# Eight tiles with packed weights for the upper half of K, the lower half by natural weights that on-chip copies between partitions bring

## The chip, the cores and the metric

The kernel runs on one core of one Trainium2 chip. The metric is the device time of one execution in microseconds (us). "Before" took 235.51 us in three runs (235.48 to 235.56). A core has TensorE (called PE in the profile; PEld is its weight loading), VectorE (DVE), ScalarE (ACT), GpSimd (POOL) and SyncE (SP), and 16 DMA engines that move data. SPq and ACTq in the profile are the DMA queues that SyncE and ScalarE issue into.

Kernels are compared only within the same rounds. A ratio is the mean time of one kernel's fast runs over that of the other's of the same rounds, so it is not quite the ratio of the medians that are quoted.

## The reference

```python
# x (16, 512, 1024), w (1024, 1024), b (1024), all bf16
def reference(x, w, b):
    wg = w.reshape(256, 4, 1024)               # groups of 4 neighbours along K
    mag = abs(wg)
    thr = second_largest(mag, axis=1)          # (by argsort in the original)
    wp = (wg * (mag >= thr)).reshape(1024, 1024)   # 2 of 4 kept
    return einsum("bsd,df->bsf", x, wp) + b
```

So it is a matrix product of 8192 tokens with K = 1024 and 1024 output columns, with weights that are pruned two out of four first. The tokens make 64 tiles of 128.

## The kernel before

Pruning compares four neighbours along K. This kernel does it by elementwise operations with those four on the same partition (on VectorE from 3.8 to 26.0 us). For that the weights are loaded "packed": partition q of half g holds rows g*512 + 4q + m for m = 0..3. The other order is "natural": partition p of k-tile kt holds row kt*128 + p. Both orders give a right product, if x is arranged to match.

- *Packed tiles.* The first seven token tiles are multiplied with the packed weights as soon as a piece is pruned. Their x is transposed on TensorE by an identity matrix, in the packed order.
- *Natural tiles.* The other 57 tiles use natural weights; their x comes by transposing DMA loads, so TensorE only multiplies.
- *From packed to natural.* The pruned weights are saved to DRAM in the packed order and read back in the natural one.

```python
pieces = [(0, 0, 256), (0, 256, 512), (1, 0, 256), (1, 256, 512), (0, 512, 1024), (1, 512, 1024)]
...
def save(g, c0, c1, eng="sp"):                     # packed, to DRAM
    issue(eng, scr_pk[:, g, :, c0:c1], wp[:, g, :, c0:c1])
def reload(h):                                     # natural, from DRAM
    fs = slice(h * FH, (h + 1) * FH)
    sp(nc.sync.dma_start(wp_nat[:, :, fs], scr_nat[:, :, fs]))
def transpose(t, g):                               # x of a packed tile, on TensorE
    xg = x_sb[(t, g)].rearrange("p (q m) -> p m q", m=4)
    tp = psum_t.tile([P, 4, P], bf16, name="tp")
    for m in range(4):
        pe(nc.tensor.transpose(tp[:, m, :], xg[:, m, :], ident[:]))
...
def finish(t):                                     # VectorE adds the bias, twice for a packed tile
    o = outp.tile([P, Dout], bf16, name="o")
    dve(nc.vector.tensor_tensor(o[:, FH:], ps_open.pop((t, 1))[:], bias_sb[:, FH:], op=Alu.add))
    dve(nc.vector.tensor_tensor(o[:, :FH], staged.pop(t)[:], bias_sb[:, :FH], op=Alu.add))
    issue("act", of[t * P:(t + 1) * P, :], o[:])
...
run({eng: order[eng].split() for eng in order})    # written orders of pruning and packed tiles
save(0, 0, 256); save(0, 256, 512); save(1, 0, 256); save(1, 256, 512)
load_batch(0)                                      # transposing load of natural tiles
reload(0)
reload(1)
load_batch(1)
load_batch(2)
for t in (2, 0, 3, 1, 6, 5, 4):
    finish(t)
# ... then 57 tiles of 16 matmuls of 512 columns each (8 k-tiles, 2 column halves)
```

The helper `seq` ties the calls on one engine into the order of its instructions. An issue that takes long holds back those behind it in its queue.

## Time and profile before

| what | value | where it is read |
|---|---|---|
| time | 235.51 us (235.48 to 235.56, 3 runs) | times |
| span of the profiled run | 233.2 us | page |
| TensorE busy | 98% | page |
| a 512-column matmul | 176.12 us / 816 = 0.216 us | chain of waits |
| first packed matmul | 7.01 us | timeline |
| first natural matmul | 33.46 us | timeline |

The profile page of before. The first line is busy time, share of the span and count of each engine. The next four are groups of instructions: source line, engine, operation, output<-input, shapes, count, then busy us, mean ns of one, and the idle time of TensorE just before them. The last two are the shares of the chain of work that ended last.

```profile
PE 229.5 (98%) x1184; PEld 112.8 (48%) x1184; DVE 104.2 (45%) x177; ACT 15.2 (7%) x27; POOL 0.7 (0%) x6
...
PE 98%; DVE 0%; issue 0%
PE ps L394 76%; PE ps L219 10%; PE ps L359 9%; PE ps L131 2%; PE tp L194 2%; DVE o L363 0%; DVE zeros L80 0%
...
L394 PE MATMUL ps<-wp_nat,xb 128*128 128x512 bf16 x816 | 176.3, 379 | 0.0
...
L219 PE MATMUL ps<-wp,xt 128*128 128x256 bf16 (+1 forms) x168 | 25.5, 308 | 0.0
L359 PE MATMUL ps<-wp_nat,xb 128*128 128x512 bf16 (+2 forms) x112 | 21.1, 349 | 0.0
...
L194 PE MATMUL tp<-ident,x 128*128 128x128 bf16 x56 | 5.0, 227 | 0.0
```

Every group of matmuls has 0.0 us of idle time before it, and the chain is TensorE from end to end. (A single 512-column matmul is shown as 379 ns long, but they overlap: the pace is 216 ns.) L219 are the packed matmuls, L359 and L394 the natural ones, L194 the transposes, L131 fillers that multiply zeros before any weights are there.

The timeline of TensorE before: start us, length us, what ran. Rows between those shown are further transposes and packed matmuls.

```profile
7.01 1.47 PE L219 MATMUL ps<-wp,xt 128*128 128x256 bf16 x12
...
18.31 15.31 PE L219 MATMUL ps<-wp,xt 128*128 128x256 bf16 x84
33.46 17.43 PE L359 MATMUL ps<-wp_nat,xb 128*128 128x512 bf16 x80
```

The packed tiles last until 33.46 us. The timeline of SyncE's queue shows the conversion of the weights in the meantime; the length here is how long the issue keeps the queue.

```profile
10.55 6.84 SPq L92 DMA_DIRECT2D wp_scratch<-wp  x4
17.45 5.87 SPq L244 DMA_TRANSPOSE xb<-in_x_dram  x1
23.50 9.10 SPq L184 DMA_DIRECT2D wp_nat<-wp_scratch  x2
```

Saves, one transposing load, reloads: the left half of the natural weights landed at 29.5 us, behind 26 us of packed work, and the right half at 39.0 us, behind natural work. TensorE never waits for it: its idle time before L359 and L394 is 0.0 us.

### The profile page before, as it was taken

How to read it: one execution, taken by the hardware profiler on the slowest of the kernel's cores; microseconds unless marked ns; L12 is line 12 of the kernel's file. 1: busy time of each engine (PE TensorE's matmuls, PEld its weight loads, DVE VectorE, ACT ScalarE, POOL GpSimd, SP SyncE). 2: the span in 40 equal slices, each digit the busy share in tenths (PEclk: the TensorE clock that was granted, in tenths of full speed). 3: DMA queues.
4: the chain of work that ended last, by engine and by line, in shares of the span. 5: the costliest groups of instructions: out<-in, count | busy, mean ns of one | idle time of the engine just before them, and what ended most of it. 6: DMA issues, size and time to landing. Idle time of an engine off the chain costs nothing.

```text
span 233.2 us, 2871 instructions
## 1 busy us (share of the span) xinstructions
PE 229.5 (98%) x1184; PEld 112.8 (48%) x1184; DVE 104.2 (45%) x177; ACT 15.2 (7%) x27; POOL 0.7 (0%) x6
## 2 busy tenths in 40 slices
PE   8999999999999999999999999999999999999995
PEld 5987444444444444444444444444444444444443
DVE  3999559533343244244234334334324424423434
ACT  3679000000000000000000000000000000000000
POOL 1000000000000000000000000000000000000000
PEclk9999999999999999999999999999999999999999
DMA  6999969999999952992239921697221221122122
GB/s 189 297 327 248 322 214 224 282 257 247 241 340 258 273 166 88 209 285 94 90 74 253 257 91 46 146 239 202 90 90 49 88 93 63 72 90 91 47 89 90
DMA packets 79500, 40.29 MB, mean 173 GB/s; under 512 B 60416, under 2 KB 71936, under 8 KB 79488
## 3 DMA queue, kind: packets, MB, share of 16 engines
q1 hardware_dynamic: 68208, 22.32, 43.9%
q10 hardware_dynamic: 11280, 17.80, 22.9%
q8 instruction: 9, 0.15, 0.3%
q14 instruction: 3, 0.02, 0.0%
HBM read 6.29 MB, written 18.87 MB: 108 GB/s over the span
## 4 chain that ended last, share of the span: by engine, by line
PE 98%; DVE 0%; issue 0%
PE ps L394 76%; PE ps L219 10%; PE ps L359 9%; PE ps L131 2%; PE tp L194 2%; DVE o L363 0%; DVE zeros L80 0%
## 5 line engine op out<-in xcount | busy, mean ns | idle before, releaser
L394 PE MATMUL ps<-wp_nat,xb 128*128 128x512 bf16 x816 | 176.3, 379 | 0.0
L394 PEld LDWEIGHTS <-xb 128*128 128x128 bf16 x816 | 79.8, 98 | 96.3
L363 DVE TENSOR_TENSOR o<-ps,bias_sb 128x512 bf16<-128x512 f32 (+1 forms) x116 | 74.0, 677 | 117.2 <-PE ps L394 110.8
L219 PE MATMUL ps<-wp,xt 128*128 128x256 bf16 (+1 forms) x168 | 25.5, 308 | 0.0
L359 PE MATMUL ps<-wp_nat,xb 128*128 128x512 bf16 (+2 forms) x112 | 21.1, 349 | 0.0
L219 PEld LDWEIGHTS <-xt 128*128 128x128 bf16 x168 | 16.2, 98 | 7.5
L359 PEld LDWEIGHTS <-xb 128*128 128x128 bf16 x112 | 10.4, 98 | 10.7
L233 DVE TENSOR_TENSOR o<-ps,bias_sb 128x512 bf16<-128x512 f32 x7 | 4.8, 685 | 5.1 <-PE ps L219 5.1
L131 PE MATMUL ps<-zeros 128*128 128x128 bf16 (+1 forms) x32 | 5.3, 328 | 1.0 <-DVE zeros L80 1.0
L154 ACT ACTIVATE mag<-w_sb 128x1024 bf16<-128x1024 bf16 (+1 forms) x4 | 6.0, 1488 | 1.0 <-DMA w_sb<-in_w_dram 1.0
L151 DVE TENSOR_TENSOR wp<-w_sb,mag 128x1024 bf16<-128x1024 bf16 (+2 forms) x7 | 5.4, 766 | 0.2
L151 DVE TENSOR_TENSOR mag<-mag,hi 128x1024 bf16<-128x1024 bf16 (+2 forms) x7 | 5.3, 767 | 0.2
L199 ACT COPY xt<-tp 128x256 f32<-128x256 f32 x14 | 4.9, 372 | 5.3 <-PE tp L194 5.3
L194 PE MATMUL tp<-ident,x 128*128 128x128 bf16 x56 | 5.0, 227 | 0.0
L234 DVE TENSOR_TENSOR o<-st,bias_sb 128x512 bf16<-128x512 f32 x7 | 4.8, 679 | 0.0
L131 PEld LDWEIGHTS <-zeros 128*128 128x128 bf16 x32 | 3.0, 125 | 2.6 <-issue 1.7
L194 PEld LDWEIGHTS <-x 128*128 128x128 bf16 x56 | 4.0, 117 | 0.4 <-DMA x<-in_x_dram 0.2
L228 ACT COPY st<-ps 128x512 f32<-128x512 f32 x7 | 3.6, 609 | 0.1
L151 DVE TENSOR_TENSOR hi<-mag 128x512 bf16<-128x512 bf16 (+1 forms) x6 | 3.0, 507 | 0.0
L151 DVE TENSOR_TENSOR lo<-mag 128x512 bf16<-128x512 bf16 (+1 forms) x6 | 3.0, 508 | 0.0
L161 DVE TENSOR_SCALAR mag<-w_sb 128x1024 uint16<-128x1024 uint16 x2 | 0.9, 427 | 2.9 <-DMA w_sb<-in_w_dram 2.9
L151 DVE TENSOR_TENSOR hi<-hi,lo 128x256 bf16<-128x256 bf16 (+1 forms) x6 | 2.0, 336 | 0.2
(11 smaller groups left out, 6.4 us busy)
## 6 DMA issues: line engine op xcount, KB each, us to landing
out_dram<-o ACTq DMA_DIRECT2D x58, 256.0 KB, 3.9
wp_nat<-wp_scratch SPq DMA_DIRECT2D x2, 1024.0 KB, 6.4
x<-in_x_dram SPq DMA_DIRECT2D x5, 256.0 KB, 5.0
out_dram<-o ACTq DMA_DIRECT2D x10, 128.0 KB, 1.7
w_sb<-in_w_dram SPq DMA_DIRECT2D x4, 256.0 KB, 4.3
w_sb<-in_w_dram SPq DMA_DIRECT2D x2, 512.0 KB, 7.1
wp_scratch<-wp SPq DMA_DIRECT2D x4, 256.0 KB, 5.6
wp_scratch<-wp ACTq DMA_DIRECT2D x2, 512.0 KB, 5.2
```

Of the source, the lines that this page charges most:

```text
L131: pe(nc.tensor.matmul(warm_ps[:, :rep * P], lhsT=zeros[:], rhs=zeros[:, None, :].to_broadcast([P, rep, P]), start=True, stop=True))
L151: dve(nc.vector.tensor_tensor(out, a, b_, op=op))
L154: act(nc.scalar.activation(self.mag[:], self.w, Act.Abs))
L194: pe(nc.tensor.transpose(tp[:, m, :], xg[:, m, :], ident[:]))
L199: act(nc.scalar.copy(xt[:].bitcast(fp32), xpk[(t, g)][:].bitcast(fp32)))
L219: pe(nc.tensor.matmul(ps[:, c0 - h * FH:c1 - h * FH], lhsT=xpk[(t, g)][m], rhs=wp[:, g, m, c0:c1], start=(new and m == ms.start), stop=(le ...
L228: act(nc.scalar.copy(st[:], ps_open.pop((t, 0))[:]))
L233: dve(nc.vector.tensor_tensor(o[:, FH:], ps_open.pop((t, 1))[:], bias_sb[:, FH:], op=Alu.add))
L234: dve(nc.vector.tensor_tensor(o[:, :FH], staged.pop(t)[:], bias_sb[:, :FH], op=Alu.add))
L359: pe(nc.tensor.matmul(ps, lhsT=xt[:, kt, :], rhs=wp_nat[:, kt, c0:c1], start=(kt == 0), stop=(kt == KT - 1)))
L363: dve(nc.vector.tensor_tensor(o[:, c0:c1], ps, bias_sb[:, c0:c1], op=Alu.add))
L394: pe(nc.tensor.matmul(pss[h][:], lhsT=xt[:, kt, :], rhs=wp_nat[:, kt, h * FH:(h + 1) * FH], start=(kt == 0), stop=(kt == KT - 1)))
```

## The change

The intent is to take work from TensorE, which has none to spare. A packed tile costs transposes that a natural tile doesn't (56 for the seven tiles of before, 5.0 us of busy time). If the packed tiles use packed weights for the upper half of K only (g = 0) and natural weights for the lower half, then half of their transposes go. To keep TensorE busy while the rest of the weights are pruned and converted, there are eight such tiles instead of seven, and three natural tiles ("lead" tiles) begin with their upper half. The detour through DRAM was judged too slow for that (my estimate), so natural weights are copied from partition to partition on the chip. The upper-half sums are staged out of PSUM, in which the kernel has six buffers for sums: ScalarE copies 16 halves, GpSimd adds the bias to them, and VectorE later adds the staged half to the lower-half product.

The diff, cut to its core (cuts are marked `...`; the written orders of instructions and the loops over the natural tiles are left out):

```diff
-    NPK = 7
+    NPK = 8
+    LEAD = 3
...
-    def save(g, c0, c1, eng="sp"):
-        issue(eng, scr_pk[:, g, :, c0:c1], wp[:, g, :, c0:c1])
-    def reload(h):
-        fs = slice(h * FH, (h + 1) * FH)
-        sp(nc.sync.dma_start(wp_nat[:, :, fs], scr_nat[:, :, fs]))
+    def spread(g, c0, c1, eng="sp"):
+        for k in range(4):
+            issue(eng, wp_nat[:, 4 * g + k, c0:c1], wp[32 * k:32 * k + 32, g, :, c0:c1])
...
-    pieces = [(0, 0, 256), (0, 256, 512), (1, 0, 256), (1, 256, 512), (0, 512, 1024), (1, 512, 1024)]
+    pieces = [(0, 0, 256), (0, 256, 512), (0, 512, 768), (0, 768, 1024), (1, 0, 512), (1, 512, 1024)]
...
-    save(0, 0, 256)
-    ...
-    load_batch(0)
-    reload(0)
-    reload(1)
+    xnat = load_nat(NPK, NPK + LEAD, 0)        # transposing load, lead tiles, all of K
+    spread(0, 0, Dout)                         # upper half of K, natural
+    xnat.update(load_nat(0, NPK, 1))           # transposing load, packed tiles, lower half of K
+    spread(1, 0, FH)                           # lower half, left columns
+    spread(1, FH, Dout)                        # lower half, right columns
+    load_batch(0)
+    pruned = const.tile([P, 1], bf16)
+    pool(nc.gpsimd.tensor_copy(out=pruned[:], in_=wp[:, 1, 3, Dout - 1:]))   # after the last pruned piece
+    for tok in order["act"].split():
+        if tok[0] == "S":
+            t, h = map(int, tok[1:].split("h"))
+            st = staged[(t, h)]
+            pool(nc.gpsimd.tensor_tensor(st[:], st[:], bias_sb[:, h * FH:(h + 1) * FH], op=Alu.add))
...
+    for h in range(2):
+        for j in range(LEAD):
+            open_nat(j, h)                     # 6 PSUM groups, upper half: 24 matmuls
+    for t in ((NPK + 0, 0), (NPK + 1, 0), (NPK + 2, 0)):
+        close(*t)
+    for t in range(3):
+        close(t, 0)
+    for j in range(LEAD):
+        close(NPK + j, 1)
+    for t in range(3):
+        close(t, 1)
+    for t in range(3, NPK):
+        close(t, 0)
+        close(t, 1)
```

`close` multiplies the lower half into a PSUM group and lets VectorE add the bias (lead tiles) or the staged half (packed tiles). GpSimd goes in the order in which ScalarE staged the halves, which is not the order of the closings.

## The prediction

> **What bounds the kernel now.** TensorE. The page gives PE 98% of the 233.2 us span, and the chain of waits is PE from 0.99 to 230.5 us without a gap. A 512-column matmul costs 0.216 us in the chain (176.12 us for 816), a 256-column one 0.109; 64 tiles need 221 us. What remains is 7.2 us before the first packed matmul, 2.1 us of transposes after it (the chain's pieces at 8.5, 10.2, 12.0, 13.2, 15.2 and 18.3 us) and 2.7 us at the end. The granted clock is 1.0.
>
> **What the change does.**
> - Matmul columns: the same.
> - Transposes on TensorE: 56 become 32; after the first packed matmul 36 become 16. Saved: about 1.2 us, all on the critical path.
> - Start: the first packed matmul still waits for the first weight piece (pruning begins at 3.8 us, its product at 6.5). No gain.
> - The 2 MB write to DRAM and the 2 MB read back become 2 MB of copies between partitions. That path wasn't critical, but its result is needed sooner: packed work ends at about 22 us, not 33.6.
> - Evacuation: VectorE's two adds per packed tile stay; ScalarE gets 16 stage copies instead of 7 (0.51 us each); GpSimd gets 16 additions of bias to staged halves, which start only after the last pruned piece (26.0 us before, about 26.5 now, estimate).
>
> **New waits.**
> 1. At 22 us: natural upper-half weights. Their pruning ends at about 16 us, as four 256-column pieces do now; four copies of 256 KB follow (a 1 MB reload landed in 6.4 us). Stall 0 to 1 us.
> 2. At 27 us (22 plus 24 matmuls): lower-half weights, left columns. Pruned at about 21.6 us, but their copies queue behind a transposing load of half of K for eight tiles (a five-tile one kept the queue 5.9 us). Landing 28 to 30; stall 0.5 to 2 us.
> 3. GpSimd. [...] The additions are not in the order of the closings: the right half of tile 1 is fifteenth on GpSimd, but is closed much earlier. [...] VectorE drains in order, and six PSUM buffers let TensorE run on to about 41 us. [...]
>
> **Predicted.** 235.5 - 1.2 + about 1.5 (between none and 3.5) = 235.8 us; 233.8 to 238.6 should hold it 8 times in 10. Faster by over 2%: 0.02; within 2%: 0.93; slower by over 2%: 0.05.
>
> **What would show it.** Transposes: count 32, about 2 us of the chain. The first packed matmul at 7.0 to 7.3 us, the first natural one at 22 us. Idle TensorE time before natural matmuls, released by a weight copy (22 and 27 us) or by VectorE (36 to 45 us); VectorE waiting for GpSimd at tiles 0, 1 and 2; mean of a GpSimd addition. From 50 us on the timeline must repeat 3.45 us per tile.
>
> **What would make it wrong.** [...] an earlier start: then about 234.3. [...] Copies between partitions far below the rate of the reload would hold TensorE at 22 us. ScalarE's stage copies may delay the later pruning, and with it everything above.

The sum came to 235.8 us (235.5 - 1.2 + 1.5). The size of the third wait, GpSimd's, was an estimate from a figure that no trace shows. The forecast took this wait to contain the first two and did not add it.

## The result, and the profile after

| | before | after |
|---|---|---|
| time, median | 235.53 us (235.48 to 235.65, 4 runs) | 238.39 us (238.21 to 238.73, 4 runs) |
| ratio | 1 | 1.0122 (95%: 1.0105 to 1.0140) |
| span of the profiled run | 233.2 us | 236.9 us |
| first packed matmul | 7.01 us | 8.37 us |
| first natural matmul | 33.46 us | 23.23 us |

The verdict is "same" at 2%, as was predicted, and the time lies within the range, close to its upper end. The changed kernel is 1.2% slower, clear of the noise; its forecast was 0.3 us slower.

The page of after, as above:

```profile
PE 227.5 (96%) x1150; PEld 112.0 (47%) x1169; DVE 104.4 (44%) x177; ACT 17.4 (7%) x30; POOL 18.7 (8%) x23
...
PE 85%; SPq 6%; DVE 4%; DMA 3%; issue 1%
...
L331 PE MATMUL ps<-wp_nat,xb 128*128 128x512 bf16 (+1 forms) x957 | 207.1, 375 | 3.9 <-DMA wp_nat<-wp 2.9
...
L327 POOL TENSOR_TENSOR st<-st,bias_sb 128x512 f32<-128x512 f32 x16 | 17.9, 1164 | 0.0
...
L335 DVE TENSOR_TENSOR o<-ps,st 128x512 bf16<-128x512 f32 x16 | 10.1, 684 | 3.8 <-POOL st L327 2.9
...
L182 PE MATMUL tp<-ident,x 128*128 128x128 bf16 x32 | 2.5, 220 | 1.8 <-DMA x<-in_x_dram 1.8
```

TensorE is no longer the whole chain: SyncE's queue (6%), VectorE and DMA have entered it. The natural matmuls now have 3.9 us of idle time before them, 2.9 of it ended by a copy of weights. (19 of the 976 natural matmuls are missing from this trace, which may make up the other 1.0 us.) The transposes are 32 with 2.5 us of busy time, where before had 56 with 5.0.

The timeline of TensorE after. In brackets: the idle time before the row and what ended it.

```profile
7.33 0.64 PE L182 MATMUL tp<-ident,x 128*128 128x128 bf16 x8 [1.84 <-DMA x<-in_x_dram]
...
8.37 1.25 PE L204 MATMUL ps<-wp,xt 128*128 128x256 bf16 x10
...
23.23 0.81 PE L331 MATMUL ps<-wp_nat,xb 128*128 128x512 bf16 x3
25.23 4.69 PE L331 MATMUL ps<-wp_nat,xb 128*128 128x512 bf16 x20 [1.19 <-DMA wp_nat<-wp]
30.72 0.68 PE L331 MATMUL ps<-wp_nat,xb 128*128 128x512 bf16 x2 [0.79 <-DMA wp_nat<-wp]
31.91 0.38 PE L331 MATMUL ps<-wp_nat,xb 128*128 128x512 bf16 x1 [0.51 <-DMA wp_nat<-wp]
32.71 17.64 PE L331 MATMUL ps<-wp_nat,xb 128*128 128x512 bf16 x79 [0.42 <-DMA wp_nat<-wp]
```

TensorE waits at 24.0 us for the last upper-half copy, and three times from 29.9 to 32.7 us for the lower-half copies of the left columns. After 32.71 us there is no further wait. The queue of SyncE in the same run:

```profile
8.42 6.86 SPq L305 DMA_TRANSPOSE xb<-in_x_dram  x1
16.82 4.48 SPq L95 DMA_DIRECT2D wp_nat<-wp  x4
21.34 5.49 SPq L305 DMA_TRANSPOSE xb<-in_x_dram  x1
26.93 6.13 SPq L95 DMA_DIRECT2D wp_nat<-wp  x8
```

The copies of the upper half are issued from 16.82 us on and land, asked one by one, at 20.8, 22.4, 23.6 and 25.2 us. The next row is the transposing load of the packed tiles, which holds the queue for 5.49 of the 9.1 us from its issue to its landing. Only then, at 26.93 us, is the first lower-half copy issued, although VectorE had pruned that piece at 22.5 us. The left columns land at 30.7, 31.0, 31.9 and 32.7 us: the first, third and fourth of these are the ends of the three waits above.

How full is the path while the upper-half copies run? The profile by stretch, from 17 to 22 us: length, then busy time (and count) of PE, PEld, DVE, ACT and POOL, granted clock, DMA share, GB/s moved. This is before:

```profile
17.00:22.00 5.00, 5.00 (x47) 4.25 (x45) 4.90 (x8) 4.88 (x9) 0.00 (x0) 1.00 1.00 230
```

And this is after:

```profile
17.00:22.00 5.00, 5.00 (x48) 4.48 (x46) 4.33 (x7) 5.00 (x8) 0.00 (x0) 1.00 0.74 128
```

The DMA engines are busy for 74% of the time, but they move only 128 GB/s. That is a hint that the copies themselves are slow, not that they wait. Their own times, from issue to landing, in the view of the tile of natural weights:

```profile
DMA to landing us min/median/max: 4.0/5.2/5.6
```

Now the row of GpSimd's additions in its timeline after:

```profile
27.81 17.85 POOL L327 TENSOR_TENSOR st<-st,bias_sb 128x512 f32<-128x512 f32 x16
```

And the row of VectorE's timeline after in which it adds the later ones of these staged halves:

```profile
44.58 7.43 DVE L335 TENSOR_TENSOR o<-ps,st 128x512 bf16<-128x512 f32 x12 [2.93 <-POOL st L327]
```

VectorE does wait 2.93 us for GpSimd, as feared, but no TensorE wait follows. The first PSUM buffer is free at 44.58 + 0.69 = 45.27 us (0.69 us is one such addition). By a count of matmuls from 32.71 us on, at 0.2158 us each, TensorE needs it at about 45.9 us (estimate). So this limit stays hidden by about 0.6 us.

**Where the time went.** From the starts of the rows above, the span splits into three terms. The second takes the packed matmuls away at 0.109 us for 256 columns and 0.216 us for 512 (24.3 us before, 14.0 after). The third takes the natural ones away (912 x 0.2158 = 196.8 us before, 960 x 0.2158 = 207.2 us after).

| term | before | after | difference |
|---|---|---|---|
| start to first packed matmul | 7.01 | 8.37 | +1.4 |
| packed stretch without its matmuls (transposes) | 2.1 | 0.9 | -1.2 |
| natural stretch to the end without its matmuls (waits, end) | 2.9 | 6.5 | +3.5 |
| sum | | | +3.7 = 236.9 - 233.2 |

(The profiled run of before was its fastest, 234.98 us, and that of after its slowest, 238.73, so this difference is larger than that of the medians, 2.9 us.)

The transposes gave what they should within their stretch. The waits took three times as much, and the start is late as well. The rest is about why the waits are so long, and whether the start matters.

### The profile page after: what moved, and what is told of

Read it like the earlier page. It is cut to its first block, busy times and chain, and to the rows that moved or that the text cites. A ratio compares the mean times of both kernels' runs of the same rounds, so it can differ in the third digit from the quotient of the medians.

```text
span 236.9 us, 2844 instructions
## 1 busy us (share of the span) xinstructions
PE 227.5 (96%) x1150; PEld 112.0 (47%) x1169; DVE 104.4 (44%) x177; ACT 17.4 (7%) x30; POOL 18.7 (8%) x23
## 4 chain that ended last, share of the span: by engine, by line
PE 85%; SPq 6%; DVE 4%; DMA 3%; issue 1%
PE ps L331 85%; SPq L95 4%; SPq L305 2%; DMA w_sb<-in_w_dram 2%; DMA wp_nat<-wp 1%; DVE hi L148 1%; DVE wp L148 1%; DVE lo L148 1%; DVE mag L148 1%; DVE mag L158 0%; DVE o L335 0%
## 5 line engine op out<-in xcount | busy, mean ns | idle before, releaser
L331 PE MATMUL ps<-wp_nat,xb 128*128 128x512 bf16 (+1 forms) x957 | 207.1, 375 | 3.9 <-DMA wp_nat<-wp 2.9
L331 PEld LDWEIGHTS <-xb 128*128 128x128 bf16 x976 | 94.9, 98 | 116.1 <-issue 4.2
L327 POOL TENSOR_TENSOR st<-st,bias_sb 128x512 f32<-128x512 f32 x16 | 17.9, 1164 | 0.0
L204 PE MATMUL ps<-wp,xt 128*128 128x256 bf16 x128 | 14.5, 273 | 0.0
L204 PEld LDWEIGHTS <-xt 128*128 128x128 bf16 x128 | 12.4, 98 | 1.4
L335 DVE TENSOR_TENSOR o<-ps,st 128x512 bf16<-128x512 f32 x16 | 10.1, 684 | 3.8 <-POOL st L327 2.9
L213 ACT COPY st<-ps 128x512 f32<-128x512 f32 x16 | 8.4, 625 | 0.2 <-PE ps L204 0.2
L182 PE MATMUL tp<-ident,x 128*128 128x128 bf16 x32 | 2.5, 220 | 1.8 <-DMA x<-in_x_dram 1.8
L187 ACT COPY xt<-tp 128x256 f32<-128x256 f32 x8 | 2.7, 375 | 5.9 <-PE tp L182 5.9
L322 POOL COPY pruned<-wp 128x1 bf16<-128x1 bf16 x1 | 0.2, 187 | 26.4 <-DVE wp L148 26.4
L148 DVE TENSOR_TENSOR hi<-hi 128x256 bf16<-128x256 bf16 (+1 forms) x6 | 2.0, 332 | 0.0
```

The lines of the kernel that those rows point to most:

```text
L148: dve(nc.vector.tensor_tensor(out, a, b_, op=op))
L187: act(nc.scalar.copy(xt[:].bitcast(fp32), xpk[t][:].bitcast(fp32)))
L204: pe(nc.tensor.matmul(ps[:, c0 - h * FH:c1 - h * FH], lhsT=xpk[t][:, m, :], rhs=wp[:, g, m, c0:c1], start=(new and m == ms.start), stop=(l ...
L213: act(nc.scalar.copy(st[:], ps_open.pop((t, h))[:]))
L327: pool(nc.gpsimd.tensor_tensor(st[:], st[:], bias_sb[:, h * FH:(h + 1) * FH], op=Alu.add))
L331: pe(nc.tensor.matmul(ps, lhsT=xt[:, kt, :], rhs=wp_nat[:, kt, c0:c1], start=(kt == first), stop=(kt == last)))
```

## The experiments

Where the expectations name theories by letters, A is the one that I held, and B and C are its rivals, with what each expects. In short, my theory was that the natural weights arrive late, because of the copies and their place in one queue behind a transposing load, and that this hides the start and GpSimd.

### 1. GpSimd in the order of the closings

```diff
-    for tok in order["act"].split():
-        if tok[0] == "S":
-            t, h = map(int, tok[1:].split("h"))
+    closing = [(t, h) for h in range(2) for t in range(3)] + [(t, h) for t in range(3, NPK) for h in range(2)]
+    for t, h in closing:
```

> Only the order of GpSimd's 16 additions changes: it becomes the order in which the staged halves are closed. In the profile of the changed kernel VectorE waits 2.9 us for GpSimd (at 41.7 to 44.6 us), but TensorE has no wait after 32.7 us. Theory A (the late copies hide GpSimd's pacing: the PSUM buffers reach just far enough, with some 0.6 us to spare): VectorE's wait disappears, the time stays at 238.4 us, within 0.4. Rival B (my prediction's third stall is real and reaches TensorE): 2 to 3 us faster, 235.5 to 236.4.

Measured: 238.22 us (237.90 to 240.44, 4 runs) against 235.59 us for before; ratio 1.0131 (1.0086 to 1.0177). The slowest run had a mean granted clock of 0.993, the other three 1.0. VectorE's wait for GpSimd shrinks from 2.93 us to 0.2 us and the time stays. So GpSimd's order, which I had thought to be one of three causes, isn't what binds here. In this run the first packed matmul came at 7.44 us, 0.9 us earlier than in the profile of after, and TensorE still resumed only at 24.74 us (25.23 in after): a first sign that the late start is hidden.

### 2 and 3. The lower-half copies on ScalarE's queue

```diff
-    spread(1, 0, FH)
-    spread(1, FH, Dout)
+    spread(1, 0, FH, "act")
+    spread(1, FH, Dout, "act")
```

> The eight copies of the lower-half weights are issued by ScalarE (free from 24.7 us) and not by SyncE, whose queue was held by the issue of the transposing load from 21.3 to 26.8 us, while the left half was pruned at 22.5. Theory A (the held queue causes the stall at 30 us): the first copy is issued near 24.8 and lands near 28.5, the closings start about 2 us earlier; but then GpSimd's order binds (0.6 us to spare), so the whole gains only 0.5 to 1.2 us: 237.2 to 237.9. Rival B (the DMA engines are full with the transposing load until 28.5 us, whichever queue issues): landing stays at 30 to 32.6 us, time 238.4 within 0.4. Rival C (no limit behind it): 2 us, 236.4.

> Both edits of the two runs before. Theory A: the gain is more than the sum of the two alone, about 2 us: 236.2 to 236.8, with no wait of VectorE for GpSimd. If the copies do not come earlier from ScalarE: 238.4. If the two simply add: the sum of the two gains.

Measured: 245.28 us (244.19 to 245.91), ratio 1.0407 (1.0373 to 1.0441); with GpSimd's order changed as well, 244.88 us (244.11 to 246.70), ratio 1.0405. Both are much worse. ScalarE's queue in the timeline of experiment 2:

```profile
23.55 0.64 ACTq L95 DMA_DIRECT2D wp_nat<-wp  x1
...
24.22 16.30 ACTq L95 DMA_DIRECT2D wp_nat<-wp  x7
```

And two rows of TensorE's timeline in the same run, with the first and the longest of its waits for these copies:

```profile
32.36 4.91 PE L331 MATMUL ps<-wp_nat,xb 128*128 128x512 bf16 x22 [1.46 <-DMA wp_nat<-wp]
...
42.60 1.87 PE L331 MATMUL ps<-wp_nat,xb 128*128 128x512 bf16 x4 [2.72 <-DMA wp_nat<-wp]
```

The left copies were issued 3.4 us earlier than in after, yet the last of them landed at 32.3 us instead of 32.7: they took 5.6 to 6.8 us from issue to landing (2.8 to 3.8 in after), and the transposing load issued before them landed only at 32.5 us. So the second queue gained 0.4 us of the 3.4. The profile counts all queues on the same 16 engines, and their share stands at 1.24 from 25 to 30 us; that the load and the copies hold each other up there is my reading.

The large loss has another source, and it makes the edit less clean than I meant it to be. With the copies gone from SyncE's queue, the next large transposing load moved up (issued at 27.3 us, landed at 40.0). The last two right-column copies were issued only at 32.6 and 40.0 us and landed at 39.5 and 42.6. Each of these two issues comes 0.02 us after a transposing load has landed (32.54 and 39.95 us). That these issues waited for the load is an inference from the times. Also, all four runs of experiment 2 had a mean granted clock of 0.986 to 0.993. Theory A, in the form "the copies are late because of their place in the queue alone", falls.

### 4. What a copy costs by itself

Into the kernel before, late, where nothing waits: three unused copies that read 32 neighbouring partitions each, as the change does, then three that read all 128; 256 KB each.

```diff
+        if bi == len(batches) - 2:
+            for k in range(3):
+                issue("sp", d32[:, k, :], wp[32 * k:32 * k + 32, 0, :, :])
+            for m in range(3):
+                issue("sp", d128[:, m, :], wp[:, 0, m, :])
```

> The kernel before, with six dead copies of 256 KB each late in the run, when the DMA engines are mostly idle: three as the change makes them (32 source partitions spread over 128), then three from 128 partitions to the same 128. In the changed kernel the four upper-half copies landed 1.1 to 1.7 us apart (about 180 GB/s of 256 KB each). Theory A (a copy that reads only 32 partitions is limited by how these are read): the first three land 1.2 us or more apart, the other three 0.7 us or less. Rival B (the copies were slow because of other traffic): both kinds land 0.6 to 0.8 us apart, at the pace of the issue. The time of the kernel stays at 235.5 within 0.5.

One look, without timing (235.55 us, correct). The first three landed at 161.3, 163.2 and 165.4 us, so 1.9 and 2.2 us apart. The other three landed at 165.8, 167.2 and 167.8 us, so 0.4, 1.4 and 0.6 us after the one before. The direction is that of a slow read from 32 partitions. But a transposing load and output stores ran at the same time (300 GB/s in all and a DMA share of 0.95 from 158 to 168 us, so the engines were not mostly idle as expected), and the sizes aren't clean. It wasn't enough to settle it.

### 5 and 6. Other source partitions (wrong result)

Each copy still reads 32 partitions, with the same bytes and the same destination, but every fourth partition instead of 32 neighbours. The rows then land in the wrong places, and the result is wrong (relative error 1.12). Nothing else changes.

```diff
-            issue(eng, wp_nat[:, 4 * g + k, c0:c1], wp[32 * k:32 * k + 32, g, :, c0:c1])
+            issue(eng, wp_nat[:, 4 * g + k, c0:c1], wp[k::4, g, :, c0:c1])
```

Experiment 6 has this edit and that of experiment 1 together.

> Wrong result on purpose: each of the 12 copies reads every fourth of the 128 partitions in place of 32 neighbouring ones; sizes, rows, queue, order and destinations are the same. Theory A ([...] the four upper-half copies, the transposing load behind them and the lower-half copies behind that are each late): the four upper-half copies, which took 8.4 us from first issue to last landing, take 5 to 6 us, TensorE's waits for weight copies at 24 and at 30 to 32.7 us shrink from 2.9 us recorded to below 1. GpSimd's order then binds (as in the theory of run e1), so the time gains 0.5 to 1.5 us only: 237 to 238. Rival B (copies between partitions are slow whichever are read): no change, 238.4 within 0.3.

Theory A holds that a copy from 32 neighbours is slow because of the partitions that it reads; how much faster the others would be was an estimate.

> The run before plus GpSimd's additions in the order of the closings; wrong result on purpose as there. Theory A (two limits one behind the other): 1.5 us or more faster than that run, 234.8 to 236. If GpSimd's order never mattered (rival): the same as that run.

The stretch from 17 to 22 us of experiment 5 (columns as above):

```profile
17.00:22.00 5.00, 5.00 (x48) 4.48 (x46) 4.36 (x7) 5.00 (x8) 0.00 (x0) 1.00 0.81 228
```

It is 228 GB/s in place of 128, with almost the same DMA share. Not all of the 228 is the copies: the next transposing load is issued within the stretch, at 19.66 us. The copies' own times are cleaner:

```profile
DMA to landing us min/median/max: 2.8/3.0/3.2
```

The four upper-half copies, issued from 16.9 us on, landed 2.8 to 3.2 us after their issue (4.0 to 5.6 in after), the last at 22.2 us in place of 25.2. From the first landing to the last it is 2.3 us in place of 4.4. So here the partitions that are read decide the rate, and the first term of the delay is shown. Three copies of 256 KB in 4.4 and in 2.3 us are about 180 and 340 GB/s (estimates from these landings), a factor of 1.9. In both runs a transposing load had been issued before the last landings, so the figures aren't exact. Why 32 neighbours are read more slowly, the traces don't show.

But the time of experiment 5 is 238.56 us (237.04 to 239.83), ratio 1.0128 (1.0072 to 1.0183), much like after. Two rows of TensorE's timeline show why:

```profile
29.00 14.03 PE L331 MATMUL ps<-wp_nat,xb 128*128 128x512 bf16 x63 [0.24 <-DMA wp_nat<-wp]
45.30 7.03 PE L331 MATMUL ps<-wp_nat,xb 128*128 128x512 bf16 x24 [2.26 <-DVE o L335]
```

And so does the stretch from 46 to 48 us, with its granted clock (third column from the end):

```profile
46.00:48.00 2.00, 2.00 (x6) 0.73 (x5) 2.00 (x4) 0.00 (x0) 0.00 (x0) 0.50 1.23 201
```

The copies cost only 0.24 us now. TensorE comes to the packed tiles' closings earlier, and there the hidden limit binds: VectorE waits for GpSimd (7.1 us in three waits), and TensorE waits 2.26 us for VectorE. After that wait the granted clock is low until past 48 us (0.50 from 46 to 48 us, 0.80 from 48 to 50, then 1.0), which costs more time. (This is the profile of one run, the slowest.) Two of the four runs had a mean granted clock of 0.993 and took 239.5 and 239.8 us; the two at 1.0 took 237.0 and 237.6. So at the full clock the faster copies alone gave about 1 us. The copies and the waits for them are as theory A expected. Of the times, only the two at the full clock lie within the 237 to 238 us expected; the median doesn't.

With both edits, experiment 6, the time is 235.11 us (234.62 to 235.69), ratio 0.9992 (0.9966 to 1.0018), and TensorE from the first natural matmul on is one unbroken stretch:

```profile
22.22 30.05 PE L330 MATMUL ps<-wp_nat,xb 128*128 128x512 bf16 x136
```

So there were two limits, one behind the other. Taking away the second alone gave nothing that is clear of the noise (experiment 1), the first alone about 1 us at best, both about 3 us (from a ratio of 1.0122 to one of 0.9992). A part of the last figure may be the start: the profiled run of experiment 6 has its first packed matmul at 7.04 us, that of experiment 5 at 8.13 us.

A correct version would have to pack the groups onto every fourth partition in the first place. No run tries it: an attempt did not build.

### 7. An earlier start

Only TensorE's order: the two transposes whose x lands late come after the first four packed matmuls.

```diff
-            "T6a F1 T7a F8 T1a T0a F10 M6.0y M7.0y M0.0y M1.0y M7.0x T5a T4a M0.0x M6.0x M1.0x "
+            "T6a F1 T7a F8 F10 M6.0y M7.0y T1a T0a M0.0y M1.0y M7.0x T5a T4a M0.0x M6.0x M1.0x "
```

> TensorE's order alone: the first two tiles' matmuls come before the transposes of tiles 1 and 0, whose load landed 0.4 us after the first pruned weights were ready in one profile, and did not in another. Theory A (the natural weights' copies set the time at which TensorE goes on at 25 us, so an earlier start only makes that wait longer): 238.2 within 0.4. Rival B (the late start adds to the time): 0.6 to 1.2 us faster, 237.1 to 237.7.

Measured: 238.36 us (238.12 to 238.43), ratio 1.0120 (1.0105 to 1.0135), no change. The first packed matmul came at 6.97 us, 1.4 us earlier than in after. The first natural one came at 22.98 us, only 0.25 us earlier, because the transposes now stand in the packed stretch, and TensorE resumed at 24.89 us after a wait for a copy. The late start is real but costs nothing as long as the copies are later still.

### 8. The repair: the queue split up

This is a correct kernel. Its changes: the upper-half copies go column half by column half, so that the left ones are issued at 14.4 us; the bias load moves behind them; the transposing load of the packed tiles is split into 3 and 5 tiles, with the left lower-half copies in between; and the edits of experiments 1 and 7.

```diff
-    spread(0, 0, Dout)
-    xnat.update(load_nat(0, NPK, 1))
+    spread(0, 0, FH)
+    spread(0, FH, Dout)
+    sp(nc.sync.dma_start(bias_sb[:], b.partition_broadcast(P)))
+    ...                                   # xb_pk: one buffer for both parts
+    load_low(0, 3)
     spread(1, 0, FH)
+    load_low(3, NPK)
     spread(1, FH, Dout)
```

> A repair that keeps the result right: upper-half copies by column halves (left columns are pruned by 11.7 us), the bias load behind them, the transposing load of the packed tiles' lower K half in two parts (tiles 0 to 2 ahead of the lower-half copies, 3 to 7 behind the left ones), GpSimd in the order of closings, TensorE's early start. Theory A (what TensorE waits for is the order and length of one DMA queue): the wait at 24 us is gone, that at 30 us below 1.5 us: 235.3 to 236.8. If the order of the queue doesn't matter (rival: the copies are limited by when weights are pruned): 238.

Measured: 236.11 us (235.75 to 236.39), ratio 1.0025 (1.0008 to 1.0043): 2.3 us faster than after, as theory A expected. Of the waits for natural weights one is left:

```profile
23.17 11.49 PE L339 MATMUL ps<-wp_nat,xb 128*128 128x512 bf16 x51
35.17 17.21 PE L339 MATMUL ps<-wp_nat,xb 128*128 128x512 bf16 x79 [0.51 <-DMA wp_nat<-wp]
```

SyncE's queue in the same run:

```profile
14.42 5.98 SPq L95 DMA_DIRECT2D wp_nat<-wp  x8
...
21.09 1.97 SPq L314 DMA_TRANSPOSE xb<-in_x_dram  x1
23.16 2.82 SPq L95 DMA_DIRECT2D wp_nat<-wp  x4
```

The copies still read 32 neighbours, but the last of the upper half lands at 22.5 us (25.2 in after). The left ones of the lower half stand behind an issue of 1.97 us in place of 5.49; they are issued from 23.16 us on and land at 26.8 to 29.3. The early issue alone can't be what helps: in experiment 2 they were issued from 23.55 us on and landed only at 29.8 to 32.3. What differs is the transposing load issued ahead of them: three tiles here, landed at 26.4 us, eight tiles there, landed at 32.5. So the other part of the delay is what was issued before the copies: its hold on the queue (1.97 us, 5.49 in after) and the time until it has landed. How much each of the five edits gives isn't known; those of experiments 1 and 7 gave nothing alone.

### 9 and 10. Other first loads, without and with the repair

In the trace of after, the second weight piece landed at 8.1 us (6.8 before), and in a stretch from 4.0 to 4.5 us the DMA engines moved only 131 GB/s (303 before). Not every profile is like that: with the same order of loads the piece landed at 6.7 us in experiment 6. The edit loads the weights and the larger pieces of x in another order, so that this hole is filled, and renumbers the packed tiles to match. Experiment 10 adds the edits of experiment 8, except the one of experiment 7, and the second part of the split transposing load comes last, behind the right lower-half copies.

```diff
     load_w(0, 0, 256)
-    load_x(7, 8, "act")
+    load_x(6, 7, "act")
-    load_x(6, 7)
-    load_x(0, 2)
-    load_w(0, 256, 512)
     load_x(4, 6)
-    load_w(0, 512, 1024)
     load_x(2, 4)
+    load_w(0, 256, 512)
+    load_x(0, 2)
+    load_w(0, 512, 1024)
+    load_x(7, 8)
```

> Only which tiles the start loads, and in which pieces, goes back to what the kernel before does: one tile on ScalarE's queue, then two pairs of tiles ahead of the second weight piece, in place of two single tiles and one pair; the tiles change roles accordingly. In every profile of the changed schedule so far the DMA engines moved only some 60 to 130 GB/s around 4.0 to 4.5 us, and the second weight piece landed at 6.7 to 8.1 us, against 6.9 in the kernel before. Theory A (the loads' pieces make the hole; with it go pruning and copies, not only TensorE's start): no hole, first packed matmul at 7.0 to 7.3 us, pruning and copies about 1 us earlier, time 237.2 to 237.8. Rival B (the start does not matter at all, as the run with TensorE's early order alone showed): 238.3. Rival C (the hole is not due to these pieces): hole and time as before.

> Right result: the repairs of the split queue (upper-half copies by column halves, bias behind them, lower K half of the packed tiles in two parts, now with the right lower-half copies ahead of the second part), GpSimd in the order of closings, and the start loads of the run before. Theory: no wait of TensorE from the first packed matmul at 7.1 us on; the time is the kernel before less the 1.2 us of transposes, 234.3 to 235.0. If the split-queue run's 236.1 owed its last 1.5 us to something other than the start: 235.6 to 236.1.

Experiment 9: 238.67 us (237.62 to 239.66), ratio 1.0118 (1.0089 to 1.0147). The hole is gone (236 GB/s from 4.0 to 4.5 us), but the second weight piece is no earlier (8.2 us), for from 6 to 8 us the rate was only 199 GB/s. That is a miss; why the first loads are slow in some profiles stays open.

Experiment 10: 236.07 us (235.19 to 236.27, 6 runs), ratio 1.0016 (0.9996 to 1.0036). That is a miss: 234.3 to 235.0 was expected if only the start was left. The natural stretch begins at 24.24 us and has no wait at all, but the start is worse:

```profile
5.84 0.62 PE L181 MATMUL tp<-ident,x 128*128 128x128 bf16 x4 [0.72 <-DMA x<-in_x_dram]
6.25 1.06 PE L126 MATMUL ps<-zeros 128*128 128x128 bf16 x8
7.11 1.06 PE L181 MATMUL tp<-ident,x 128*128 128x128 bf16 x8
7.96 1.27 PE L126 MATMUL ps<-zeros 128*128 128x128 bf16 x10
9.03 1.60 PE L203 MATMUL ps<-wp,xt 128*128 128x256 bf16 x10
```

Compare 7.33 us in after, where eight transposes took 0.64 us and not 1.06. From the start of the row to that of the next, those eight transposes and the ten fillers took 0.85 and 1.07 us here, 0.48 and 0.56 in after. So TensorE ran at about half that speed here, and the ten packed matmuls from 9.03 us on still took 1.60 us (1.25 in after); it had been idle for 0.72 us before 5.84. That the idle time caused it isn't shown: in the profile of experiment 9, with the same first loads and an idle 0.91 us, eight transposes took 0.61 us, and in that of experiment 11, with no idle time, eight took 1.06 us at 5.34 us. The profile's granted clock is 1.0 in all of these stretches, so that column doesn't show it. When full speed is reached differs from profile to profile (eight transposes took 0.64 us at 5.25 us in before, 1.06 at 7.11 us here), for a reason that stays open.

### 11. The copies alone, in the kernel before

The kernel before with copies instead of the detour through DRAM, nothing else.

```diff
-    save(0, 0, 256)
-    ...
+    spread(0, 0, FH)
+    spread(1, 0, FH)
     load_batch(0)
-    reload(0)
-    reload(1)
+    spread(0, FH, Dout)
+    spread(1, FH, Dout)
```

> One part of the change alone: the kernel before, seven tiles packed over all of K, with its natural weights made by the same copies between partitions and not through DRAM. Its natural work begins at 33.6 us. Theory A (the copies are no faster, but the time for them is the point: here they have 10 us more): 235.5 within 0.4. Rival B (copies between partitions disturb whatever runs): 1 us or more slower.

Measured: 235.52 us (235.34 to 235.72), ratio 0.9999 (0.9979 to 1.0020). The slow copies are harmless here, where the natural work begins at 33.93 us (23.23 in after), so about 10 us more of packed work cover them.

### 12. The repair, with fillers in the start

The first loads of experiment 9, the queue of experiment 10 with the bias load moved behind the left lower-half copies, and fillers spread between the first transposes, so that TensorE isn't idle in the start.

```diff
-            "T6a F1 T5a F8 T4a T3a F10 M6.0y M5.0y ...       (order of experiment 10)
+            "T6a F8 T5a T4a F6 T3a F4 M6.0y M5.0y ...
```

> Right result: the run with split queue and start loads, with TensorE's filler matmuls moved (eight between the first two transposes in place of one, then six and four in place of eight and ten), and the bias load put where the queue is idle, ahead of the right lower-half copies. In that run no matmul waited for weights from 24.2 us on, but its first packed matmul came at 9.0 us and not at 7.1: TensorE had idled 0.7 us before tile 5's load landed, and ran the eight fillers, eight transposes and ten fillers after it at about half speed. Theory A (only the late start is left): first packed matmul at 7.1 to 7.4 us, natural work from about 22.5, some 1.2 to 1.7 us faster than that run: 234.3 to 235.0, a little faster than the kernel before. Rival B (pruning and copies, not TensorE's start, set the end there too): waits for copies come back at 25 and 28 us, time 235.5 to 236.1.

Measured: 235.15 us (234.85 to 235.65, 6 runs) against 235.44 us (11 runs); ratio 0.9983 (0.9953 to 1.0012). So it is even with before, or slightly faster by less than the noise; it missed its expectation by a little. TensorE:

```profile
7.30 1.07 PE L203 MATMUL ps<-wp,xt 128*128 128x256 bf16 x8
8.89 0.38 PE L203 MATMUL ps<-wp,xt 128*128 128x256 bf16 x2 [0.52 <-DVE wp L147]
...
23.09 29.09 PE L339 MATMUL ps<-wp_nat,xb 128*128 128x512 bf16 x131
```

The natural stretch has no wait. What is left of the loss is in the packed stretch, where pruning waits for the second weight piece, which landed at about 8.1 us as in after.

### All of them by the three terms

The three terms of the result section, as differences to before in the profiled runs (us; the packed matmuls are 14.0 us and the natural ones 207.2 us in each):

| kernel | start | packed stretch | natural stretch | sum | ratio of times |
|---|---|---|---|---|---|
| after | +1.4 | -1.2 | +3.5 | +3.7 | 1.0122 |
| 1, GpSimd's order | +0.4 | -0.5 | +3.5 | +3.4 | 1.0131 |
| 7, earlier start | 0.0 | -0.1 | +3.5 | +3.4 | 1.0120 |
| 5, other source partitions | +1.1 | -1.0 | +4.7 | +4.8 | 1.0128 |
| 6, both (wrong result) | 0.0 | -0.9 | +0.4 | -0.4 | 0.9992 |
| 8, split queue | +0.2 | -0.1 | +1.1 | +1.2 | 1.0025 |
| 10, with first loads | +2.0 | -0.9 | +0.1 | +1.3 | 1.0016 |
| 12, with fillers | +0.3 | -0.3 | +0.1 | +0.1 | 0.9983 |

Each row is one profile. The kernel before itself isn't fixed to half a microsecond: in the profiles of experiments 4 and 11, which have its start, the first packed matmul came at 7.6 us and not at 7.01.

The start and the packed stretch trade: what an earlier start gains, the packed stretch gives back, because pruning (and with it the loads) sets when packed work can go on (in experiment 12 TensorE waits 0.52 us for it). Both repaired kernels 10 and 12 and the wrong one, 6, have no wait of note left in the natural stretch, and none of them gets below before by more than 0.4 us.

## Why the prediction was right or wrong

The class and the range were right, the range by only 0.2 us. The forecast was 235.8 us and the result 238.39, so the sum was 2.6 us too low. The mechanism of the stalls was right, but they were mis-sized: 3.5 us in place of 1.5, which is 2.0 of the 2.6. The rest lies, as far as single profiles tell, in the saving: start and packed stretch together were to give 1.2 us, and in the profiled runs they took 0.2 us more than before. (That is 1.4 us; 0.8 goes off, because the two profiled runs lie further apart than the medians.)

1. *"Transposes: ... Saved: about 1.2 us, all on the critical path."* Right in the count and, in after, in the size: the packed stretch without its matmuls went from 2.1 to 0.9 us. "All on the critical path" is not borne out, as far as single profiles tell. In after TensorE then waited for copies. Where the start is nearly on time and the result right (experiments 7, 8 and 12), the packed stretch is only 0.1 to 0.3 us shorter than before: it then contains waits for pruned weights or for transposed x (0.52 us for pruning in experiment 12). Only the wrong kernel 6 had a start on time and kept 0.9 us.
2. *"Stall 0 to 1 us" at 22 us, for the upper-half copies.* Right in place and cause, too small: TensorE stopped after three natural matmuls, so at about 23.9 us, and went on at 25.23, which is 1.35 us. I took the rate of the copies from the reload from DRAM ("a 1 MB reload landed in 6.4 us"). They took 8.4 us, from the first issue at 16.82 us to the last landing at 25.2. They were also issued 0.8 us later than forecast, because the pruning ended at 16.8 us and not at 16. Experiment 5 shows why they were slow, the 32 neighbouring partitions. The prediction had named this only among what could make it wrong ("copies between partitions far below the rate of the reload").
3. *"Landing 28 to 30; stall 0.5 to 2 us" for the lower half.* Right in cause (the copies "queue behind a transposing load"), too early: they landed at 30.7 to 32.7 us, and the stall is the other 2.2 us of the 3.5. The slow upper-half copies hold up the transposing load, and this the lower-half copies, so the same error counts twice: in experiment 5, with faster copies, the load was issued at 19.66 us and not at 21.34, and the left copies landed at 26.4 to 29.7 us. Also the piece was pruned at 22.5 us and not at 21.6. Experiment 8, beside experiment 2, shows that the transposing load ahead of them has a large part in it (landed at 26.4 and at 32.5 us, the copies from 26.8 and from 29.8 us on).
4. *The sum "about 1.5 (between none and 3.5)".* This is the step that failed: the two stalls measured 3.5 us, the upper end of what I had allowed. I had put in a middle value, as if the two were unlikely to be late together, though one leads to the other. The late start doesn't change this: when experiment 7 brought the first packed matmul back to 6.97 us, the natural stretch stayed at +3.5 and the packed stretch lost what the start had gained.
5. *GpSimd: "The additions are not in the order of the closings".* Right: an addition took 1.16 us, and VectorE's wait of 2.93 us for them is there. The wait did not reach TensorE in after, by about 0.6 us, because the copies had delayed TensorE by more than I thought; in experiment 5, without that delay, it did (2.26 us).
6. *"The first packed matmul at 7.0 to 7.3 us."* Wrong: 8.37 us, because TensorE waits for x (1.84 us). The x of eight tiles and the weights come in another order, and in this profile the first loads landed later; with the same order experiment 6 started at 7.04 us, so a part of it is the run. An earlier start alone gave nothing (experiment 7). In the repaired kernels, where the copies no longer hold TensorE, late first loads are what is left of the loss (experiment 12).
7. *"From 50 us on the timeline must repeat 3.45 us per tile."* Right: no further wait after 32.71 us.

The size of the best case is worth a look. With all waits gone, experiment 6 is 0.4 us below before, not 1.2. The best correct version, experiment 12, is 0.3 us below before, and neither is clear of the noise. The removed cost was small to begin with, and the slack that the long packed stretch had given to pruning and copies was what paid for it.

What stays open: why the first loads of the changed kernel land late in some profiles and not in others (the second weight piece from 6.7 us in experiment 6 to 8.1 in after, in the same order), when TensorE reaches full speed in the start, whether a correct packing onto every fourth partition is possible, and how much of experiment 2's loss is the order of the transposing loads and how much the late issue of its last copies.

## What to carry to other kernels

When work is taken from the engine that bounds the kernel, the slack of everything beside it shrinks by the same time: list what is needed at the new, earlier moment, follow its chain through one queue, and add delays that cause each other instead of averaging them. Cost a copy between partitions by a measured copy that reads the same partitions, not by the rate of another transfer: here 256 KB landed 4.0 to 5.6 us after the issue from 32 neighbours and 2.8 to 3.2 us from every fourth partition (after and experiment 5). And issuing a copy earlier on another queue need not land it earlier: in experiment 2 the copies were issued 3.4 us earlier and the last landed 0.4 us earlier, behind a transposing load that landed at 32.5 us. An edit that gives nothing alone may be one of two limits in series, so try both together before it is dropped.
